# An attention and MLP chain on one core: h = x2 @ w_in by one level of Strassen's scheme

## The chip, the cores and the metric

The kernel runs on one core of one Trainium2 chip. The metric is the device time of one execution in microseconds; a time is the median over several executions. A profile is taken of one execution, which has a time of its own.

## The reference, cut to what matters

```python
# attention: 32 heads (4 batches x 8), 576 tokens, head size 64, causal, with a cumulated bias
scores = q @ k.T / 8 + minimum(bias, 0);  attn = softmax(scores);  x = attn @ v    # x: 2304 x 512
c  = (x @ w1) * (x @ w2)              # 2304 x 1024
x2 = (c @ w3) @ w_out                 # 2304 x 512, w3 1024 x 1024, w_out 1024 x 512
h  = x2 @ w_in                        # 2304 x 2048, w_in 512 x 2048
g  = h - tanh(h)
out = g @ w_out2                      # 2304 x 512, w_out2 2048 x 512
```

All inputs are float64 in memory.

## The kernel before, in words

Every engine's instruction order is written out by a planner inside the program: `pl.op` notes an operation with the engines that may run it, its reads, its writes and a priority (a lower number is taken first); `order` plays the list through with assumed costs and puts each operation on an engine; `emit` then issues all in that order. On the chip each engine runs its instructions in order and waits on semaphores. The assumed costs, the biases and the priorities are in `PARAM`. All DMAs are issued from SP's queue (L392).

**Precision.** A float32 product is made of three matmuls on "fp32r" operands: each operand is split (`split`, L404) into a rounded high part (`copy`: ScalarE L395 or VectorE L396) and a low part (`sub`: VectorE L399 or GpSimd L401), and high*high, high*low and low*high are added in a bank. So a block of 128 rows, depth 128 and n columns costs three matmuls of n columns. A float64 weight tile of 128x512 is turned into float32 by `assemble` (L490: one ScalarE or VectorE operation, L495 or L496, then L497, L498, L500 and L502 on VectorE); `convert` does that and splits, `lay_by` does that and writes the float32 tile to DRAM, `fetch` brings it back and splits.

**Stages.** (1) The heads (L621), with the products x @ w1 and x @ w2 (`products`, L791; c goes to DRAM) in between as filler: block j of 512 tokens may run when its heads are done. (2) w3 @ w_out (L865 to L875, eight rounds of 24 matmuls, `wah` and `wal` are its result), after the conversions of 8 tiles of w_out and 16 of w3. The first six rounds (`wlast=6`) have a priority ahead of the remaining products. (3) x2 = c @ (w3 w_out) (L890 to L917) in five blocks of tokens, four of 512 and one of 256: c is loaded (`cf`) and split, and each block takes 4 banks of 24 matmuls. Its result is split out of PSUM and written to DRAM as high and low parts. In the same stretch the 16 tiles of w_in are converted into `wih` and `wil`, which stay in SBUF, and those of w_out2 into `voh` and `vol`. (4) h and out (L925 to L974): five blocks of tokens as before; for each of 16 slices f of 128 columns of h there are 12 matmuls into one of 4 banks (L945), then the gate g = h - tanh(h), then for each 128 tokens of the block three matmuls of 512 columns (L966 to L968) into one of the other 4 banks, one slice or more later.

The gate of a slice: ScalarE squares h out of PSUM (L953), squares again (L954), takes tanh (L955) and a mask (L958); VectorE makes h*u out of PSUM (L956), a polynomial (L957), h - tanh out of PSUM (L959), a predicated copy (L960); then the split into `gh` (L396) and `gl` (L401, GpSimd).

Of the kernel before, what the change touches and what calls it, by code (L numbers as in the profile page):

```python
# [9 lines left out]
F32 = mybir.dt.float32  # L10
# [6 lines left out]
P = 128  # L17
# [8 lines left out]
TB = 512  # L26
# [49 lines left out]
class Plan:  # L76
# [68 lines left out]
    def order(self):  # L145
# [18 lines left out]
        def better(o, e, t):  # L164
            early = t < PARAM["early"]
            bias = {"DVE": PARAM[{"sub": "dsub", "copy": "dcopy"}.get(o.kind, "dother") + ("0" if early else "")], "ACT": PARAM["act"], "POOL": PARAM["pool"]}
# [123 lines left out]
def f_mm(n, m=P):  # L290
    return [(112.0 if m > 64 else 58.0, 227.0 if n == 512 else n * 0.447 + 4.8 if n >= 96 else 30.0)]
# [6 lines left out]
def f_pair(ns):  # L298
    f = [(112.0, 0.8333 * n + 3.5) for n in ns for _ in range(2)]
    return [(f[0][0], f[0][1] + 50.0)] + f[1:-1] + [(f[-1][0], f[-1][1] + 40.0)]  # L300
# [31 lines left out]
def tile_kernel(ctx, tc, qk, v, s, w1, w2, w3t, w_out, w_in, w_out2, out):  # L332
# [49 lines left out]
    x2_d = Buf(len(XT) * KC)  # L382
    x2_d.t = dram.tile([P, 2, KC, NT], F32, name="x2_d")

    wt_d = Buf(NF2)
# [12 lines left out]
    def sub(dst, a, b, n, r, w, prio, psum=False):  # L398
# [3 lines left out]
        pl.op(o, r=r, w=w, prio=prio, two=not psum, kind="sub")  # L402

    def split(hi, hb, lo, lb, src, n, r, prio, psum=False):  # L404
        copy(hi, src, n, r, [hb], prio, psum)
        sub(lo, src, hi, n, r + [hb], [lb], prio, psum)
# [60 lines left out]
    wip = Pool("wip", "left")  # L467
    wih = wip.buf("wih", [P, KC, DF2], F32R, n=16)
    wil = wip.buf("wil", [P, KC, DF2], F32R, n=16)
    cp = Pool("cp", "right")  # L470
    cf_r = cp.ring("cf", PARAM["ncf"], [P, 512])
    x2s_r = cp.ring("x2s", 3, [P, 2, 512], F32R, n=2)
# [4 lines left out]
    voh = [(pre if f < NPRE else p2).buf(f"voh{f}", [P, DM], F32R) for f in range(NF2)]  # L477
    vol = [(pre if f < NPRE else p2).buf(f"vol{f}", [P, DM], F32R) for f in range(NF2)]
    x2b = [q_.buf(f"x2b{i}", [P, 2, KC, BLK], F32R) for i, q_ in enumerate((pre, p2))]
    gh_r = p2.ring("gh", PARAM["ng"], [P, BLK], F32R)  # L480
    gl_r = p2.ring("gl", PARAM["ng"], [P, BLK], F32R)
    u_r = p2.ring("u", 2, [P, BLK])
    sq_r = p2.ring("sq", 2, [P, BLK])
    th_r = p2.ring("th", 2, [P, BLK])
    pg_r = p2.ring("pg", 2, [P, BLK])
    mk_r = p2.ring("mk", 1, [P, BLK])
# [3 lines left out]
    def assemble(src, prio, first=None, after=()):  # L490
        r_, t_ = raw_r.next(), t1_r.next()
# [18 lines left out]
    def lay_by(i, src, prio, after=()):  # L510
        t_ = assemble(src, prio, None, after)
        dma(lambda: wt_d.t[i], lambda: t_.t.bitcast(F32), P * 2048, [t_], [(wt_d, i)], prio)
# [7 lines left out]
    keep.open()  # L520
    w12.open()
    abp.open()
# [313 lines left out]
    products(0)  # L836
    for b in range(1, B):
# [6 lines left out]
        if b == B - 1:  # L844
# [3 lines left out]
            wtmp.open()  # L848
        for j in range(NB):
            if b * S < min((j + 1) * TB, NT) <= (b + 1) * S:  # L850
                products(j)
    abp.close()
    w12.close()
    wip.open()


# [164 lines left out]
```

## Time and profile before

| what | value |
|---|---|
| median of 3 executions | 930.7 us (930.68 to 930.79) |
| the profiled execution | 931.48 us |
| its span, first to last instruction | 929.8 us |
| TensorE busy / weight loads | 921.6 us (99%) / 765.1 us (82%) |
| VectorE, ScalarE, GpSimd busy | 700.5 us (75%), 426.6 us (46%), 377.8 us (41%) |
| data moved | 115.36 MB, 124 GB/s over the span |

Busy time of TensorE counts each matmul from its start to a modelled end, and matmuls overlap, so a busy engine may still be issuing more slowly than it could. The distance from start to start is what one costs. VectorE's instructions overlap a little as well.

### The profile page before, as it was taken

What the parts mean: (1) busy time and instruction counts of PE and PEld (TensorE: products, weight loads), DVE (VectorE), ACT (ScalarE), POOL (GpSimd) and SP (SyncE); (2) the same over time, 40 slices, a digit from 0 to 9 for tenths busy, and PEclk for the clock granted to TensorE, in tenths of its full rate; (3) what the DMA queues carried; (4) which work ended last, traced back from release to release, by engine and by line L of the source; (5) the groups of instructions that cost most, each with busy time, mean ns of one, the idle gap of its engine ahead of it and who ended that gap; (6) DMA issues with size and microseconds to landing.
All of it is one profiled execution on the core that took longest, in us unless ns stands there. A gap on an engine that the chain in (4) does not pass through costs nothing.

```text
span 929.8 us, 14217 instructions
## 1 busy us (share of the span) xinstructions
PE 921.6 (99%) x5007; PEld 765.1 (82%) x5007; DVE 700.5 (75%) x1485; ACT 426.6 (46%) x952; POOL 377.8 (41%) x309
## 2 busy tenths in 40 slices
PE   9999999999999999999999999999999999999998
PEld 7777878888887888899888988888888888888887
DVE  8999897876664299996789999997556655656665
ACT  7857565655551022211423275554444444444353
POOL 2256765545342044414978544452222222222221
PEclk9999999999999999999999999999999999999999
DMA  7666646654421144477897652221020001100010
GB/s 226 183 199 181 201 146 205 213 160 135 131 84 49 56 147 155 164 233 240 284 326 247 227 176 68 75 107 46 1 91 15 31 1 46 46 1 0 1 47 23
DMA packets 58888, 115.36 MB, mean 124 GB/s; under 512 B 5713, under 2 KB 24305, under 8 KB 58818
## 3 DMA queue, kind: packets, MB, share of 16 engines
q1 hardware_dynamic: 58818, 114.47, 38.6%
q8 instruction: 39, 0.64, 0.3%
q14 instruction: 31, 0.25, 0.1%
HBM read 85.30 MB, written 25.46 MB: 119 GB/s over the span
## 4 chain that ended last, share of the span: by engine, by line
PE 92%; DVE 4%; POOL 1%; issue 1%; ACT 1%; DMA 1%; POOLq 0%; DVEq 0%
PE bank L945 21%; PE bank L806 20%; PE bank L966 7%; PE bank L967 7%; PE bank L968 7%; PE bank L725 5%; PE bank L752 4%; PE bank L908 4%; PE bank L909 4%; PE bank L907 4%; PE bank L670 2%; PE bank L671 2%; PE bank L668 2%; PE bank L872 1%; PE bank L871 1%; PE bank L870 1%
## 5 line engine op out<-in xcount | busy, mean ns | idle before, releaser
L401 POOL TENSOR_TENSOR gl<-pg,gh 128x512 fp32r<-128x512 f32 (+1 forms) x78 | 99.2, 1272 | 260.9 <-DVE gh L396 249.0
L945 PE MATMUL bank<-x2b,wih 128*128 128x512 f32 (+1 forms) x640 | 181.3, 368 | 0.0
L945 PEld LDWEIGHTS bank<-x2b,wih 128*128 128x128 f32 x640 | 117.0, 188 | 21.2
L958 ACT ACTIVATE mk<-u,const 128x512 f32<-128x512 f32 (+1 forms) x80 | 54.5, 681 | 142.5 <-DVE pg L960 142.4
L945 PE MATMUL bank<-x2b,wil 128*128 128x512 f32 (+1 forms) x320 | 117.7, 368 | 0.0
L966 PE MATMUL bank<-voh,gh 128*128 128x512 f32 x288 | 112.2, 390 | 0.0
L967 PE MATMUL bank<-vol,gh 128*128 128x512 f32 x288 | 112.2, 390 | 0.0
L968 PE MATMUL bank<-voh,gl 128*128 128x512 f32 x288 | 112.0, 389 | 0.0
L691 ACT ACTIVATE e<-e,nmx 128x576 f32<-128x576 f32 (+4 forms) x160 | 89.2, 559 | 39.7 <-DVE nmx L685 38.8
L956 DVE TENSOR_TENSOR pg<-bank,u 128x512 f32<-128x512 f32 (+1 forms) x80 | 50.9, 636 | 42.3 <-POOL gl L401 42.3
L685 DVE CUSTOM_DVE_ANT_0 e<-bank,msk 128x288 f32<-128x288 f32 (+4 forms) x160 | 64.3, 422 | 16.5 <-PE bank L671 14.2
L725 PE MATMUL bank<-ident,e 128*128 128x128 f32 (+1 forms) x480 | 75.4, 276 | 0.6 <-ACT e L691 0.3
L396 DVE CAST gh<-pg 128x512 fp32r<-128x512 f32 (+1 forms) x77 | 30.5, 396 | 52.8 <-PE bank L967 52.6
L945 PEld LDWEIGHTS bank<-x2b,wil 128*128 128x128 f32 x320 | 60.3, 188 | 9.9
L401 POOL TENSOR_TENSOR xl<-cf,xh 128x512 fp32r<-128x512 f32 (+1 forms) x40 | 53.3, 1360 | 34.2 <-DVE xh L396 32.3
L953 ACT ACTIVATE u<-bank 128x512 f32<-128x512 f32 (+1 forms) x80 | 43.7, 546 | 50.4 <-PE bank L945 42.3
L395 ACT ACTIVATE en<-bank 128x256 f32<-128x256 f32 (+3 forms) x97 | 40.9, 427 | 52.2 <-PE bank L725 42.3
L495 ACT ACTIVATE wt<-wraw 128x512 f32<-128x512 f32 x54 | 36.4, 673 | 59.4 <-DMA wraw<-w_in 26.7
L968 PEld LDWEIGHTS bank<-voh,gl 128*128 128x128 f32 x288 | 54.1, 188 | 11.4
L966 PEld LDWEIGHTS bank<-voh,gh 128*128 128x128 f32 x288 | 54.2, 188 | 10.8
L967 PEld LDWEIGHTS bank<-vol,gh 128*128 128x128 f32 x288 | 54.1, 188 | 10.5
L806 PE MATMUL bank<-xh,w1h 128*128 128x512 f32 (+1 forms) x160 | 62.7, 392 | 0.0
(134 smaller groups left out, 2280.2 us busy)
## 6 DMA issues: line engine op xcount, KB each, us to landing
rqk<-qk SPq DMA_DIRECT2D x24, 576.0 KB
wraw<-w_out SPq DMA_DIRECT2D x24, 512.0 KB
wraw<-w SPq DMA_DIRECT2D x16, 512.0 KB
c_d<-cst SPq DMA_DIRECT2D x32, 256.0 KB
wraw<-w3t SPq DMA_DIRECT2D x16, 512.0 KB
wraw<-w_in SPq DMA_DIRECT2D x16, 512.0 KB
cf<-c_d SPq DMA_DIRECT2D x32, 256.0 KB
x_d<-x2s SPq DMA_DIRECT2D x16, 512.0 KB
```

The source lines that it names most:

```text
L401: o.append(("POOL", c_pool2(n), lambda: nc.gpsimd.tensor_tensor(dst(), a(), b().bitcast(F32), op=ALU.subtract)))
L685: nc.vector.tensor_tensor_reduce(e.t[:nq, EOFF[t] + k0:EOFF[t] + k1], bk.t[:nq, :k1 - k0], bi.t[:nq, bo + k0:bo + k1], -0.125, 3.0e38 if f ...
L691: act(lambda: nc.scalar.activation(et(), et(), AF.Exp, bias=nmx.t[:nq, i, tm:tm + 1], scale=-1.0, accum_out=ssum.t[:nq, pj, t, i:i + 1]), ...
L725: nc.tensor.transpose(bk.t[:rows, (at + m) * P:(at + m + 1) * P], e.t[:, EOFF[t] + c * P:EOFF[t] + c * P + rows], ident.t)
L806: nc.tensor.matmul(bk.t[:, :w], w_.t[:, k, f * P:(f + 1) * P], x_.t[:, k, :w], start=k == 0 and i == 0, stop=k == KC - 1 and i == 2)
L945: nc.tensor.matmul(bk.t[:, :w], w_.t[:, k, a], X2.t[:, i, k, :w], start=k == 0 and n == 0, stop=k == KC - 1 and n == 2)
L953: act(lambda u=u, hp=hp, c_=c_: nc.scalar.activation(c_(u), hp(), AF.Square), w, [bk], [u], pr, psum=True)
L956: dve(lambda u=u, pg=pg, hp=hp, c_=c_: nc.vector.tensor_tensor(c_(pg), hp(), c_(u), op=ALU.mult), w, [bk, u], [pg], pr)
L958: act(lambda u=u, mk=mk, c_=c_: nc.scalar.activation(c_(mk), c_(u), AF.Relu, bias=const.t[:, 1:2]), w, [u, const], [mk], pr, extra=93.0)
L966: nc.tensor.matmul(bank[n].t, gh.t[:, a], voh[f].t, start=f == 0, stop=False)
L967: nc.tensor.matmul(bank[n].t, gh.t[:, a], vol[f].t, start=False, stop=False)
L968: nc.tensor.matmul(bank[n].t, gl.t[:, a], voh[f].t, start=False, stop=f == NF2 - 1)
```

## The change

The products of h are taken over pairs of 384-token blocks (three pairs of 768 tokens). For such a pair, the depth 512 of x2 is cut in two, the 2048 columns of w_in in two, and the tokens in two; the eight block products become seven (Winograd's form of Strassen's scheme). The operands of a product are sums and differences of quarters. In detail:

- **w_in.** Its 16 tiles are put into float32 and laid by in DRAM (`wi_d`) with a priority behind the heads, and later read back, added and subtracted, split (56 splits of 128x256) and written to `ws_d`. That is spread over the eight rounds of w3 @ w_out (`weights(i)`). In the h stage each step loads its seven operands, 256 KB each, into a ring `ws` of 13.
- **x2.** Six blocks of 384 tokens in place of five; its result leaves PSUM as it is. The operands of the first pair are made at once (8 differences, 14 splits); x2 of the other pairs goes to DRAM (`xf_d`), is read back in the h stage (`later_x2`), combined, split and written to `x2_d`, and loaded again.
- **h and out.** A step (3 pairs x 8) makes seven products of 6 matmuls of 384 columns, issued in pairs (0 and 1, 2 and 3, 4 and 5, then 6), with the 9 out matmuls of a tile of the step before between them. Two banks hold products (three in the first step), six hold out. Sums of products are partly made in PSUM (a product is added to a bank that has been read) and partly by VectorE: five additions out of PSUM and two copies a step. The gate runs on 128x384 tiles in SBUF, four a step; h*u, h - tanh and the low part may go to VectorE or GpSimd.
- **Order.** `wlast` is 0 (all of w3 @ w_out behind the products x @ w1, x @ w2), no tile of w_out2 is laid by, 12 of its 16 tiles have buffers from before the h stage (4 so far), the rings `gh` and `gl` have 8 buffers of 384 columns (3 of 512 so far), the staging buffers of the products are used again for `cf` and for the sums, and the numbers of `PARAM` differ throughout. The planner's matmul cost is n / 2.4 + 13 ns.

```diff
-BLK = 512
-HT = [(t, min(t + BLK, NT)) for t in range(0, NT, BLK)]
-XT = [(t, min(t + 512, NT)) for t in range(0, NT, 512)]
+XB = 384
+XT = [(t, t + XB) for t in range(0, NT, XB)]
+ORDER = (0, 5, 1, 6, 4, 3, 2)
...
+    for n in range(NF2):
+        c, kg, m = n // 8, n // 4 % 2, n % 4
+        j, i = ((0, 0), (0, 1), (1, 1), (1, 0))[m]
+        k, qd = j * 2 + kg, c + 2 * i
+        lay_by(wi_d, k * 4 + qd, w_in[k * P:(k + 1) * P, qd * 512:(qd + 1) * 512], PARAM["layw"] + 10 * n)
...
+
+        def lay(i, x):
+            for m in range(2):
+                st = wst_r.next()
+                split(lambda st=st: st.t[:, :, 0], (st, 0), lambda st=st: st.t[:, :, 1], (st, 1),
+                      lambda m=m: v_(x).rearrange("p (f x) -> p f x", x=P)[:, m * 2:m * 2 + 2], 256, [x], pr, kind="late")
+                dma(lambda m=m: ws_d.t[c * 4 + m * 2:c * 4 + m * 2 + 2, :, i, kg].rearrange("f p h x -> p f h x"), lambda st=st: st.t.bitcast(F32), P * 2048,
+                    [st], [(ws_d, c * 14 + i * 2 + kg)], pr, row=1024, issue=600.0)
...
+        if part == 0:
+            a11, a21 = unit(0, 0), unit(0, 1)
+            lay(0, a11)
+            s3 = made(a11, a21)
+            lay(6, s3)
+            held_w[:] = [a11, a21, s3]
+        else:
+            a11, a21, s3 = held_w
+            a22 = unit(1, 1)
+            lay(3, a22)
+            s1 = made(a21, a22, ALU.add, a21)
+            lay(4, s1)
+            s2 = made(s1, a11, to=a11)
+            lay(5, s2)
+            a12 = unit(1, 0, s3)
+            lay(1, a12)
+            lay(2, made(a12, s2, to=a12))
...
+            x = (xd_r if p else xs_r).next()
+            held[l, d] = x
+            copy(lambda x=x, d=d: x.t, lambda d=d: bks[d].t[:, :XB], XB, [bks[d]], [x], 1.9e5, psum=True)
+            if p:
+                dma(lambda d=d: xf_d.t[p, l, d], lambda x=x: x.t, P * XB * 4, [x], [(xf_d, (p * 2 + l) * KC + d)], 2.2e5, row=1536, issue=580.0)
...
+        b11, b12, b21, b22 = b
+        lay(0, b11)
+        lay(1, b21)
+        lay(2, b22)
+        lay(4, made(b12, b11, b11))
+        lay(6, made(b22, b12, b12))
+        t2 = made(b22, b11)
+        lay(5, t2)
+        lay(3, made(b21, t2, b21))
...
+
+        def lay(i, x):
+            st = x2s_r.next()
+            split(lambda: st.t[:, 0], (st, 0), lambda: st.t[:, 1], (st, 1), lambda: x.t, XB, [x], pr, kind="xs")
+            dma(lambda: x2_d.t[p, i, :, kg], lambda: st.t.bitcast(F32), P * 2 * XB * 4, [st], [(x2_d, p * 14 + i * 2 + kg)], pr, issue=580.0)
+
+        operands(kg, b, xt_r, pr, lay)
...
+
+        def product(n, i, bk, first):
+            def mm():
+                for kg in range(2):
+                    for m, (a, z) in enumerate(((0, 0), (0, 1), (1, 0))):
+                        nc.tensor.matmul(bk.t[:, :XB], W[i].t[:, kg, a], X[i].t[:, kg, z], start=first and kg == 0 and m == 0, stop=kg == 1 and m == 2, skip_group_check=True)
...
+
+        def plus(bk, y):
+            x, v_ = tmp()
+            dve(lambda: nc.vector.tensor_tensor(v_(), bk.t[:, :XB], y[1](), op=ALU.add), XB, [bk, y[0]], [x], -1.0e6)
+            return x, v_
+
...
+            def both(o, i, a, r, w):
+                pl.op([("DVE", c_dve(XB), lambda: nc.vector.tensor_tensor(o.t, i(), a.t, op=ALU.mult if o is pg else ALU.subtract)),
+                       ("POOL", c_pool2(XB), lambda: nc.gpsimd.tensor_tensor(o.t, i(), a.t, op=ALU.mult if o is pg else ALU.subtract))], r=r, w=w, prio=pr, two=True, kind="gate")
+            act(lambda: nc.scalar.activation(u.t, h(), AF.Square), XB, [hb], [u], pr)
+            act(lambda: nc.scalar.activation(sq.t, u.t, AF.Square, bias=const.t[:, 0:1], scale=SQ_A), XB, [u, const], [sq], pr, extra=93.0)
+            act(lambda: nc.scalar.activation(th.t, h(), AF.Tanh), XB, [hb], [th], pr)
+            both(pg, h, u, [hb, u], [pg])
+            dve(lambda: nc.vector.scalar_tensor_tensor(pg.t, sq.t, SQ_K, pg.t, op0=ALU.add, op1=ALU.mult), XB, [sq, pg], [pg], pr, two=True)
+            act(lambda: nc.scalar.activation(mk.t, u.t, AF.Relu, bias=const.t[:, 1:2]), XB, [u, const], [mk], pr, extra=93.0)
+            both(th, h, th, [hb, th], [th])
+            dve(lambda: nc.vector.copy_predicated(pg.t, mk.t.bitcast(U32), th.t), XB, [mk, th], [pg], pr, two=True)
+            copy(lambda: gh.t, lambda: pg.t, XB, [pg], [gh], pr)
+            sub(lambda: gl.t, lambda: pg.t, lambda: gh.t, XB, [pg, gh], [gl], pr, psum=last, kind="gate")
+            for n in range(3):
+                o = bank[l * 3 + n]
+
+                def om(n=n, o=o):
                     a = slice(n * P, (n + 1) * P)
+                    nc.tensor.matmul(o.t, gh.t[:, a], voh[f].t, start=fp == 0 and f == fp + l * NFP, stop=False)
+                    nc.tensor.matmul(o.t, gh.t[:, a], vol[f].t, start=False, stop=False)
+                    nc.tensor.matmul(o.t, gl.t[:, a], voh[f].t, start=False, stop=fp == NFP - 1 and f == fp + (1 - l) * NFP)
+                pe(f_op(3 * f_mm(512)), om, [gh, gl, voh[f], vol[f]], [o], 2.0e6 + pos + PARAM["outlag"] + n_tile[0] % 4 * 40 + n * 12)
+            n_tile[0] += 1
...
+        product(0, 0, a, True)
+        m1 = taken(a)
+        product(1, 5, b, True)
+        u2 = plus(b, m1)
+        product(2, 1, a, False)
+        h11 = taken(a)
+        gated(h11, fp, 0)
+        product(3, 6, b, False)
+        u3 = plus(b, m1)
+        c = h_r[0].next()
+        product(4, 4, c, True)
+        h22 = plus(c, u3)
+        gated(h22, fp + NFP, 1)
+        product(5, 3, b, False)
+        h21 = plus(b, m1)
+        gated(h21, fp + NFP, 0)
+        product(6, 2, c, False)
+        h12 = plus(c, u2)
+        gated(h12, fp, 1)
```

## Rows read from the trace of the kernel before

**Rows 1.** The page: its head and the busy time of the engines.

```profile
span 929.8 us, 14217 instructions
PE 921.6 (99%) x5007; PEld 765.1 (82%) x5007; DVE 700.5 (75%) x1485; ACT 426.6 (46%) x952; POOL 377.8 (41%) x309
```

**Rows 2.** The page: the chain that ended last, shares of the span by engine.

```profile
PE 92%; DVE 4%; POOL 1%; issue 1%; ACT 1%; DMA 1%; POOLq 0%; DVEq 0%
```

**Rows 3.** The chain in order of time, h and out: start, length, what (us).

```profile
691.60 2.72 PE bank L945 x12
697.04 2.72 PE bank L945 x12
...
893.58 1.43 PE bank L945 x12
896.40 1.43 PE bank L945 x12
```

**Rows 4.** Groups by shape, TensorE: count | busy, mean | idle before.

```profile
L945 PE MATMUL bank<-x2b,wih 128*128 128x512 f32 x512 | 157.7, 389 | 0.0
...
L966 PE MATMUL bank<-voh,gh 128*128 128x512 f32 x288 | 112.2, 390 | 0.0
...
L909 PE MATMUL bank<-xh,wal 128*128 128x512 f32 x128 | 49.8, 389 | 0.0
...
L945 PE MATMUL bank<-x2b,wih 128*128 128x256 f32 x128 | 23.6, 282 | 0.0
...
L909 PE MATMUL bank<-xh,wal 128*128 128x256 f32 x32 | 9.1, 283 | 0.0
```

**Rows 5.** Busy time by stretch: columns as its head line names them, GB/s last.

```profile
150.00:292.00 142.00, 142.00 (x954) 117.03 (x953) 96.73 (x314) 75.83 (x223) 62.91 (x60) 1.00 0.48 146
292.00:323.00 31.00, 31.00 (x138) 25.65 (x137) 8.03 (x13) 0.47 (x1) 2.90 (x3) 1.00 0.16 60
323.00:433.00 110.00, 109.90 (x570) 94.30 (x569) 100.23 (x176) 24.79 (x40) 40.27 (x28) 1.00 0.59 190
433.00:532.00 99.00, 99.00 (x488) 84.14 (x487) 81.40 (x108) 31.55 (x53) 75.90 (x56) 1.00 0.78 257
549.00:866.00 317.00, 317.00 (x1403) 262.55 (x1402) 221.25 (x344) 151.17 (x259) 95.91 (x69) 1.00 0.12 40
```

**Rows 6.** Timeline of VectorE in the h stage: start, length (us), instruction.

```profile
565.91 1.51 DVE L497 TENSOR_SCALAR wt<-wt 128x512 f32<-128x512 f32 x1
567.35 0.68 DVE L956 TENSOR_TENSOR pg<-bank,u 128x512 f32<-128x512 f32 x1
567.95 0.68 DVE L959 TENSOR_TENSOR th<-bank,th 128x512 f32<-128x512 f32 x1
...
569.14 0.42 DVE L498 TENSOR_SCALAR wt<-wt 128x512 uint32<-128x512 uint32 x1
569.48 0.76 DVE L960 COPY_PREDICATED pg<-mk,th 128x512 f32<-128x512 uint32 x1
570.12 0.69 DVE L500 SCALAR_TENSOR_TENSOR wt<-wraw,wt 128x512 uint32<-128x512 uint32 x1
```

**Rows 7.** Timeline of GpSimd in the same stretch.

```profile
565.52 1.62 POOL L401 TENSOR_TENSOR gl<-pg,gh 128x512 fp32r<-128x512 f32 x1 [1.42 <-DVE gh L396]
```

**Rows 8.** Groups by shape, operations of the gate: mean ns of one.

```profile
L401 POOL TENSOR_TENSOR gl<-pg,gh 128x512 fp32r<-128x512 f32 x64 | 88.8, 1388 | 228.6 <-DVE gh L396 219.0 <-ACT gh L395 9.6
...
L954 ACT ACTIVATE sq<-u,const 128x512 f32<-128x512 f32 x64 | 46.3, 723 | 2.7 <-DVE pg L957 2.3
L959 DVE TENSOR_TENSOR th<-bank,th 128x512 f32<-128x512 f32 x64 | 44.2, 690 | 6.5 <-ACT th L955 5.0
...
L401 POOL TENSOR_TENSOR gl<-pg,gh 128x256 fp32r<-128x256 f32 x14 | 10.4, 740 | 32.3 <-DVE gh L396 30.1 <-PE bank L945 2.2
...
L954 ACT ACTIVATE sq<-u,const 128x256 f32<-128x256 f32 x16 | 8.2, 512 | 0.1
...
L959 DVE TENSOR_TENSOR th<-bank,th 128x256 f32<-128x256 f32 x16 | 6.7, 420 | 5.4 <-ACT th L955 5.4
```

More of the change, by code (lines that the diff above doesn't have):

```diff
@@ L520, in tile_kernel @@
     keep.open()
+    abp.open()
     w12.open()
-    abp.open()
     xp.open()
@@ L918, in tile_kernel @@
+    x_r = Ring(x2b)
+    X0 = {i: x_r.next() for i in ORDER}
+    for j in range(len(XT)):
+        x2_block(j)
+    for i in range(NPRE):
+        out_weights(i)
     cp.close()
@@ new lines, in tile_kernel, with later_x2 @@
+    for i in range(NPRE, NF2):
+        out_weights(i)
+    w_r, h_r, n_tile = Ring(ws), [Ring(bank[5:8])], [0]
+    def later_x2(p, kg, pr):
+        b = []
+        for z, y in ((0, 0), (0, 1), (1, 0), (1, 1)):
+            x = xt_r.next()
+            b.append(x)
+            dma(lambda x=x: x.t, lambda z=z, y=y: xf_d.t[p, y, z * 2 + kg], P * XB * 4, [(xf_d, (p * 2 + y) * KC + z * 2 + kg)], [x], pr, row=1536)
+        def lay(i, x):
[3 more added lines that the diff above has]
+        operands(kg, b, xt_r, pr, lay)
@@ new lines, in step, with tmp, taken, gated @@
+    def step(p, fp, pos, X, W):
+        pr, last = 3.0e5 + pos, p == NPAIR - 1 and fp == NFP - 1
+        def product(n, i, bk, first):
+            def mm():
+                for kg in range(2):
+                    for m, (a, z) in enumerate(((0, 0), (0, 1), (1, 0))):
+                        nc.tensor.matmul(bk.t[:, :XB], W[i].t[:, kg, a], X[i].t[:, kg, z], start=first and kg == 0 and m == 0, stop=kg == 1 and m == 2, skip_group_check=True)
+            pe(f_op(6 * f_mm(XB)), mm, [W[i], X[i]], [bk], 2.0e6 + pos + n // 2 * 45 + n % 2)
+        def tmp():
+            x = tmp_r.next()
+            return x, lambda: x.t[:, :XB]
+        def plus(bk, y):
+            x, v_ = tmp()
+            dve(lambda: nc.vector.tensor_tensor(v_(), bk.t[:, :XB], y[1](), op=ALU.add), XB, [bk, y[0]], [x], -1.0e6)
+            return x, v_
+        def taken(bk):
+            x, v_ = tmp()
+            copy(v_, lambda: bk.t[:, :XB], XB, [bk], [x], -1.0e6, psum=True)
+            return x, v_
+        def gated(src, f, l):
+            hb, h = src
@@ new lines, in step @@
+        gated(h21, fp + NFP, 0)
+        product(6, 2, c, False)
+        h12 = plus(c, u2)
+        gated(h12, fp, 1)
+        if fp == NFP - 1:
+            for l in range(2):
+                for n in range(3):
+                    ob, t0, bk = osb_r.next(), p * 2 * XB + l * XB + n * P, bank[l * 3 + n]
+                    for a, z in ((0, 256), (256, 512)) if last else ((0, 512),):
+                        copy(lambda ob=ob, bk=bk, a=a, z=z: ob.t[:, a:z], lambda bk=bk, a=a, z=z: bk.t[:, a:z], z - a, [bk], [(ob, int(a > 0))] if last else [ob], pr, psum=True)
+                    dma(lambda t0=t0: out[t0:t0 + P, :], lambda ob=ob: ob.t, P * DM * 4, [ob], [], 0)
@@ new lines, in tile_kernel @@
+    for p in range(NPAIR):
+        if p < NPAIR - 1:
+            for kg in range(2):
+                later_x2(p + 1, kg, 3.0e5 + p * NFP * 160 + PARAM["x2p"])
+        X = X0 if p == 0 else {}
+        for i in ORDER if p else ():
+            X[i] = x_r.next()
+            dma(lambda x=X[i]: x.t.bitcast(F32), lambda i=i, p=p: x2_d.t[p, i], P * 4 * XB * 4, [(x2_d, [p * 14 + i * 2, p * 14 + i * 2 + 1])], [X[i]], 3.0e5 + p * NFP * 160, issue=600.0)
+        for fp in range(NFP):
+            pos = (p * NFP + fp) * 160.0
+            if p == 0 and fp == 1:
+                h_r[0] = Ring(bank[6:8])
+            W = {}
+            for n, i in enumerate(ORDER):
+                W[i] = w_r.next()
+                dma(lambda x=W[i]: x.t.bitcast(F32), lambda i=i, fp=fp: ws_d.t[fp, :, i], P * 2048, [(ws_d, [fp // 4 * 14 + i * 2, fp // 4 * 14 + i * 2 + 1])], [W[i]], 3.0e5 + pos + n * 20, row=2048)
+            step(p, fp, pos, X, W)
```

220 lines of the change are left out of this document (109 added, 111 removed).

## The prediction

> **What bounds the kernel now.** I read the page first: TensorE is busy for 921.6 of 929.8 us [rows 1], and the chain that ended last is TensorE for 92% of its length [rows 2]. So I ask of every edit what it does to TensorE's issue, and of all other engines only whether they come late. Busy time does not say what a matmul costs, since lengths overlap (mean 389 ns at 512 columns [rows 4]). The chain in order of time does: in h and out twelve matmuls of 512 columns take 2.72 us, the next twelve of that line start 5.44 us after the first (12 of h, 12 of out), so one costs 226.7 ns; twelve of 256 columns take 1.43 us, 119.2 ns each [rows 3]. Third, the stretches: TensorE has hardly a gap after 150 us, at a granted clock of 1.00 throughout. VectorE is busy 97 of 142 us, then 8 of 31, 100 of 110, 81 of 99, and in the h stage 221 of 317 us. ScalarE has room everywhere, the DMA share is 0.78 at most and 0.12 in the h stage [rows 5].
>
> **The change: h on TensorE.** Before, h is 64 groups of twelve at 2.72 us and 16 at 1.43 us [rows 3] (the two thirds of them that read `wih` count 512 and 128 [rows 4]): 174.1 + 22.9 = 197.0 us. After, it is 3 pairs x 8 steps x 7 products x 6 = 1008 matmuls of 384 columns. That shape is not in the trace. A line through the two that are (0.42 ns a column and 11.7 ns each) gives 172.9 ns, in all 174.3 us: **22.7 us less**. The bounds are 384 columns at the 512 rate (170.0 ns: 171.4 us, 25.6 less) and at the 256 rate (178.8 ns: 180.2 us, 16.8 less). I take the line, since a fixed part per matmul explains both shapes. An eighth of the products would be 24.6 us; the shorter matmul gives 1.9 back.
>
> x2 goes from 384 matmuls of 512 columns and 96 of 256 (three lines of 128 and 32 each, as on the one shown [rows 4]) to 576 of 384: 98.5 to 99.6 us, **1.1 more** (0.6 less to 4.5 more by the same bounds). Out has the same 864 matmuls.
>
> **VectorE in the h stage.** Costs first. Back to back, two operations of 512 columns start 0.60 us apart, though each is 0.68 long; a fast one takes 0.34 to the next, a predicated copy 0.64 [rows 6]. So an operation holds VectorE for 0.09 less than its length. At 384 columns I take the mean of the lengths at 512 and 256 (0.690, 0.420 [rows 8]), 0.555, less 0.09: 0.47 us; a fast copy 0.27, a predicated copy 0.50. GpSimd's subtraction is 740 ns at 256 and 1388 at 512, waits included: about 1.0. ScalarE's square goes from 723 and 512 to 0.62 [rows 8]; its operations out of PSUM I put at 0.48, a little shorter, as an estimate from that.
>
> A step is 42 matmuls of h and 36 of out: 7.26 + 8.16 = 15.4 us of TensorE. All on VectorE, its four gates cost 4 x (3 x 0.47 + 0.50 + 0.47 for the low part + 0.27) = 10.6 us, the five additions 2.35, together 12.9. Work for the next pair (8 differences and 14 splits in 8 steps) adds 8 x 0.47 + 14 x 0.74 = 14.1 us, 1.8 a step; in the first pair the last four tiles of w_out2 (4 x 2.8 us) add 1.4. That is 16.1 us of 15.4 in the first pair, 14.7 in the second, 12.9 in the third. ScalarE can take the copies (1.1 + 0.5 of it): four gates there cost 4 x (2 x 0.62 + 2 x 0.48) = 8.8 us, the two bank copies 1.0, those copies about 3: 12.8 of 15.4. And GpSimd can work while VectorE reads PSUM, 2.35 us a step. So it fits, at 14.5 of 15.4 in the first pair before GpSimd helps: covered, but by little where before 30% was free. I charge **2 us** for the first pair.
>
> Here stands what is held against GpSimd's help. A fast operation that is 0.42 long alone is 1.51 when it meets a GpSimd subtraction, and ends 0.3 us behind it [rows 6, 7]: they exclude each other. The Trainium skill's page "SBUF — State Buffer" ("SBUF: two separate sides") says so as a rule: VectorE operations with two SBUF inputs and GpSimd's take turns on one port pair, the loser blocks fully. The gate of before reads h from PSUM in two of its operations; now h lies in SBUF and these join the excluded ones. What that can come to is the first rival.
>
> **Banks.** Two banks hold products, four so far. Products go in pairs with nine out matmuls (2.04 us) between: a bank that is finished is written again 2.04 + 1.04 = 3.1 us later. In that time one reader of 0.48 to 0.56 us has to start and end. With some 0.2 us to pass a finish on in each direction, 1 us; 2 us are left for a queue in front of it. I charge nothing and put the failure among the rivals. The out banks of a pair are written anew only a step after their last matmul, so their six copies are covered.
>
> **Start and end.** In the first step there are no out matmuls: seven products and two of the next step, 9.3 us, have to cover the first gate, which starts at 3.1 us and is some nine dependent operations of about 0.5 us: 5 us and what it waits behind other gates. I charge **1.5 us** (0 to 4). At the end, after the last product, there are still four groups of nine, 8.2 us, for a gate of 6 us: covered; after the last matmul the copies and the DMA are as before.
>
> **w3 @ w_out.** With `wlast` 0 its eight rounds (24 matmuls, 5.44 us) come behind all products, no longer mixed with them. Each needs two conversions, of which two buffers hold only two rounds' worth. On VectorE: 2 x (2 x 0.34 + 2 x 0.60 + 0.60) + 0.60 = 5.6 us a round, six rounds: 1 us late; if GpSimd takes the low parts at 1.39 and shuts VectorE out, 7.1, 10 us late. I charge **2 us** (0 to 10). The sums of w_in cost VectorE at most 56 x 0.33 + 16 x 0.60 = 28 us, w_out2's eight more conversions 20, x2's first pair 14: 62 us. What leaves this stretch is 16 conversions of w_in (30 us without the splits) and 20 low parts and some high parts out of PSUM (about 15): 17 more, and 27 us are free from 323 to 532 us [rows 5]. Its DMA: by the sizes of the tiles 8.4 MB of w_in and 9.4 of x2 go, 14.7 and 4.2 for w_in's sums and 3.1 for x2 come: 4 MB more. At 257 GB/s for a share of 0.78, 330 at full, that is 13 us on the 142 that 0.59 of 110 and 0.78 of 99 us are, of 209.
>
> **Moved into the heads:** 16 tiles laid by, 16 x 1.88 = 30 us of VectorE and 32 DMAs on SP behind those of the heads by priority. From 150 to 323 us VectorE has 68 us free [rows 5], and TensorE has the products to run: nothing, and if the heads come late, up to 2.
>
> **The loads of the h stage:** seven tiles of 256 KB a step are 1.8 MB in 15.4 us, 119 GB/s, where 257 GB/s ran at a share of 0.78 [rows 5]; the ring holds six tiles ahead, some 13 us. At a pair's change 5.5 MB of x2 come as well: with the weights 7.3 MB, 22 us at 330 GB/s, behind buffers that come free one by one; the first is loaded ahead and the last is wanted 27 us on. Nothing.
>
> **Sum:** 931.5 - 22.7 + 1.1 + 2 + 1.5 + 2 = 915.4 us for a profiled execution; the median of the runs lies 0.8 below that of the profiled one (930.7 to 931.5), so **914.6 us**.
>
> **Rivals.** (a) VectorE and GpSimd become the bound of the h stage, and it ends slower. It decides where a step reaches 16.2 us: 24 x 0.75 is the gain of 18 that the other terms leave. If GpSimd takes the 12 movable operations of a step at 1.0 and each shuts VectorE out for 0.9, the excluded work is 10.8 + 4 x (0.47 + 0.50 + 0.27) + 1.8 = 17.6 us, in the third pair 15.8: 16 x 2.2 + 8 x 0.4 = 38 us, **950 us**. For it: no free room in the first pair; against it: ScalarE and VectorE alone come to less than 15.4 in two pairs of three. 0.10. (b) The readers of the two banks come late by more than the 2 us that are left, now and then: 0.1 us on each of four handovers in 24 steps is 10 us, **924 us**. For it: in-order queues with operations of 1 us in front. 0.14. (c) The conversions hold up w3 @ w_out and so x2 (10 instead of 2) and the first step (4 instead of 1.5): **925 us**. 0.12. (d) The gain is eaten up and the time is the same: 0.04. (e) My case, 906 to 920: 0.60.
>
> **Numbers.** About 0.2% (1.9 us) is what a measurement of this kernel can tell from no change. Faster: (e), (b), (c) less a little, 0.85; same 0.04; slower 0.11. The range goes from all terms at their good ends (384 columns at the 512 rate and no stall, 905) to (b) or (c) with a little of the other, 930.
>
> **What would show it.** Right: in the h stage six matmuls of a product in 1.04 us, a step in 15.4 to 15.7 us, x2 as long as before, h and out together some 374 us for 393. Wrong: TensorE waiting for VectorE's sums or for `gh` and `gl` in every step (a, b), VectorE above 95% there; TensorE waiting for `w3h` around 390 to 430 us (c); gaps before 150 us, if the laid-by tiles hurt the heads; a matmul of 384 columns dearer than 173 ns.

## The result

The changed kernel takes 921.5 us (median of 4 runs, 920.9 to 921.9) where the kernel before takes 930.7 in the same comparison: a ratio of 0.990, 95% interval 0.988 to 0.992. It is faster, inside the range, and 6.9 us above the predicted 914.6. The profiled execution took 921.88 us with a span of 920.2.

The page of the changed kernel, its head, its busy times and the chain by engine (for [rows 1] and [rows 2]):

```profile
span 920.2 us, 15850 instructions
PE 906.6 (99%) x5174; PEld 790.6 (86%) x5174; DVE 790.7 (86%) x1884; ACT 549.0 (60%) x1292; POOL 112.1 (12%) x106
...
PE 89%; DVE 5%; DMA 3%; ACT 1%; issue 1%; SPq 0%; ACTq 0%; DVEq 0%
```

TensorE is still the bound. VectorE went from 75 to 86%, ScalarE from 46 to 60%, GpSimd from 41 to 12%. The stretches (for [rows 5]: time busy of PE, PEld, DVE, ACT, POOL, then clock, DMA share, GB/s) show where:

```profile
150.00:292.00 142.00, 142.00 (x939) 115.95 (x937) 132.71 (x403) 54.74 (x167) 66.25 (x58) 1.00 0.60 185
...
547.00:866.00 319.00, 319.00 (x1589) 287.12 (x1588) 280.62 (x579) 235.99 (x499) 0.00 (x0) 1.00 0.66 214
```

The laid-by tiles of w_in fill VectorE in the heads (133 of 142 us, 97 before) without a gap on TensorE. In the h stage VectorE is busy 281 of 319 us and GpSimd never. All that TensorE's list of waits names after 300 us is this (us in total, times, longest):

```profile
PE bank L1055 <- DMA ws<-ws_d: 1.3, 1, 1.3
PE bank L1055 <- DVE asb L1064: 1.1, 1, 1.1
PE bank L1055 <- ACT xd L410: 0.4, 1, 0.4
```

Three waits, all between the first product of h and the first matmul of out. The chain in order of time shows one later step, products in runs of 12, 12, 12 and 6 matmuls of 384 columns (for [rows 3]):

```profile
762.87 2.08 PE bank L1055 x12
...
767.04 2.10 PE bank L1055 x12
...
771.23 2.10 PE bank L1055 x12
...
776.09 1.06 PE bank L1055 x6
...
778.55 2.08 PE bank L1055 x12
```

A step is 15.68 us (762.87 to 778.55). Between the runs stand nine matmuls of out: 764.95 to 767.04 is 2.09 us for them. Uniform stretches of the same trace give 173.3 ns for 384 columns and 226.7 for 512, so 12 should take 2.08, nine 2.04, six 1.04, and the step 42 x 173.3 + 36 x 226.7 = 15.44. The matmuls that follow a change of width take longer, though nothing is waited for. By these rows (each run to the start of the next) the 36 matmuls of out take 8.34 us for 8.16 and the 42 of h 7.34 for 7.28: most of the excess lies on out.

From the starts of TensorE's stages in the two traces:

| stretch | before | after | difference | predicted |
|---|---|---|---|---|
| start to first matmul of h | 532.29 | 532.83 | +0.5 | +1.1 (x2), +2 (w3 @ w_out) |
| first of h to last matmul of out | 393.08 | 379.57 | -13.5 | -22.7, +1.5 (first step), +2 (first pair) |
| last matmul to end of span | 4.47 | 7.77 | +3.3 | 0 |
| sum | 929.84 | 920.17 | -9.7 | -16.1 |

Sixty matmuls of h stand before the first of out, which comes 14.21 us after the first of h: 10.4 us of work and 3.8 lost. Before there were 72 at 226.7 ns in 16.35 us, nothing lost.

The chain through the first step and the timeline of ScalarE at the end:

```profile
537.70 0.61 DVE wt L522
...
538.33 0.33 SPq L407
...
538.72 4.99 DMA ws<-ws_d
...
543.84 3.36 PE bank L1055 x18
```

```profile
909.42 1.34 ACT L410 ACTIVATE osb<-bank 128x256 f32<-128x256 f32 x4 [2.37 <-PE bank L1097]
912.24 1.35 ACT L410 ACTIVATE osb<-bank 128x256 f32<-128x256 f32 x4 [1.48 <-DMA out<-osb]
915.06 1.40 ACT L410 ACTIVATE osb<-bank 128x256 f32<-128x256 f32 x4 [1.46 <-DMA out<-osb]
```

At the start, SP issues a load of w_out2 (538.33) once VectorE has freed its buffer (L522, 537.70), and only behind it the operands of the next products (`ws`); the first of them lands at 543.7, and TensorE, which has issued seven products by then, waits for it. (The seven operands of the first step were issued by 500.4.) At the end two output tiles are copied out, then the copies wait 1.5 us until a tile's DMA has landed, twice.

### The profile page after: what moved, and what is told of

The parts are those of the page before. It is cut to its first block, busy times and chain, and to the rows that moved or that the text cites. A ratio compares the mean times of both kernels' runs of the same rounds, so it can differ in the third digit from the quotient of the medians.

```text
span 920.2 us, 15850 instructions
## 1 busy us (share of the span) xinstructions
PE 906.6 (99%) x5174; PEld 790.6 (86%) x5174; DVE 790.7 (86%) x1884; ACT 549.0 (60%) x1292; POOL 112.1 (12%) x106
## 4 chain that ended last, share of the span: by engine, by line
PE 89%; DVE 5%; DMA 3%; ACT 1%; issue 1%; SPq 0%; ACTq 0%; DVEq 0%
PE bank L826 21%; PE bank L1055 18%; PE bank L1096 7%; PE bank L1097 7%; PE bank L1095 7%; PE bank L745 5%; PE bank L772 5%; PE bank L979 2%; PE bank L978 2%; PE bank L980 2%; PE bank L690 2%; PE bank L688 2%; PE bank L691 2%; PE bank L941 2%; PE bank L942 2%; PE bank L943 2%
## 5 line engine op out<-in xcount | busy, mean ns | idle before, releaser
L1055 PE MATMUL bank<-x2b,ws 128*128 128x384 f32 x1008 | 192.9, 337 | 2.8 <-DMA ws<-ws_d 1.3
L1055 PEld LDWEIGHTS bank<-x2b,ws 128*128 128x128 f32 x1008 | 178.8, 188 | 12.1 <-DVE asb L1064 3.0
L711 ACT ACTIVATE e<-e,nmx 64x64 f32<-64x64 f32 (+4 forms) x160 | 89.1, 558 | 95.6 <-DVE nmx L705 95.0
L705 DVE CUSTOM_DVE_ANT_0 e<-bank,msk 64x64 f32<-64x64 f32 (+4 forms) x160 | 64.7, 420 | 4.5 <-PE bank L691 3.9
L980 PE MATMUL bank<-xh,wal 128*128 128x384 f32 x192 | 64.1, 334 | 0.0
L978 PE MATMUL bank<-xh,wah 128*128 128x384 f32 x192 | 64.1, 334 | 0.0
L979 PE MATMUL bank<-xl,wah 128*128 128x384 f32 x192 | 64.1, 334 | 0.0
L826 PE MATMUL bank<-xh,w2h 128*128 128x512 f32 (+1 forms) x160 | 63.3, 396 | 0.0
L826 PE MATMUL bank<-xh,w1l 128*128 128x512 f32 (+1 forms) x160 | 59.4, 371 | 0.0
L1087 DVE COPY_PREDICATED pg<-mk,th 128x384 f32<-128x384 uint32 x96 | 57.8, 602 | 1.9
```

The costliest lines, as they stand in the source:

```text
L705: nc.vector.tensor_tensor_reduce(e.t[:nq, EOFF[t] + k0:EOFF[t] + k1], bk.t[:nq, :k1 - k0], bi.t[:nq, bo + k0:bo + k1], -0.125, 3.0e38 if f ...
L711: act(lambda: nc.scalar.activation(et(), et(), AF.Exp, bias=nmx.t[:nq, i, tm:tm + 1], scale=-1.0, accum_out=ssum.t[:nq, pj, t, i:i + 1]), ...
L826: nc.tensor.matmul(bk.t[:, :w], w_.t[:, k, f * P:(f + 1) * P], x_.t[:, k, :w], start=k == 0 and i == 0, stop=k == KC - 1 and i == 2)
L978: nc.tensor.matmul(bk.t[:, :XB], wah.t[:, f, a], ch, start=f == 0, stop=False)
L979: nc.tensor.matmul(bk.t[:, :XB], wah.t[:, f, a], cl, start=False, stop=False)
L980: nc.tensor.matmul(bk.t[:, :XB], wal.t[:, f, a], ch, start=False, stop=f == NF - 1)
```

## The experiments

Twelve kernels were run, in four groups, each with the kernel before beside it, which lay at 930.5 to 931.1. Where no interval is given, the time is of one execution.

**The end's buffers.**

```diff
-    cst_r = abp.ring("cst", 3, [P, TB])
-    asb_r = abp.ring("asb", 4, [P, TB])
+    cst_r = abp.ring("cst", 3, [P, TB], n=2)
+    asb_r = abp.ring("asb", 4, [P, TB], n=2)
...
-                    ob, t0, bk = osb_r.next(), ...
+                    ob, t0, bk = (tmp_r if last else osb_r).next(), ...
```

> The last step's six out tiles are staged in six of the seven buffers that held the sums of the products, in place of the ring of two. Theory (the end of the changed kernel, 7.8 us from the start of the last matmul to the end of the span where it was 4.5 before, waits for the DMA of an earlier out tile to land before a staging buffer is free): the end falls to 4.5 to 5.0 us, the time to 918.2 to 918.8 us. Rival (the end is long because ScalarE makes all twelve half copies of the last block alone, 0.34 us each): nothing is gained by buffers, 7.5 us and more, 921.2 to 921.8.

919.15 us (918.7 to 919.3), ratio 0.988 (0.986 to 0.989): the end falls as the theory said, and the time lies 0.4 us above its range. ScalarE's timeline at the end:

```profile
909.75 2.02 ACT L410 ACTIVATE cst<-bank 128x256 f32<-128x256 f32 x6 [2.38 <-PE bank L1097]
911.79 2.02 ACT L410 ACTIVATE asb<-bank 128x256 f32<-128x256 f32 x6
```

The twelve copies run without a wait, and the span ends 4.83 us after the last matmul and not 7.77, as before the change (4.47). The ring of two tiles cost 2.9 of the 3.3 us.

**The order of the loads at the start.** Three of the last four conversions of w_out2 are created after the weight loads of the second step and wait for them.

```diff
-    for i in range(NPRE, NF2):
-        out_weights(i)
+    out_weights(NPRE)
...
+            if p == 0 and fp == 1:
+                for i in range(NPRE + 1, NF2):
+                    out_weights(i, [W[n] for n in ORDER])
```

> The last three conversions of w_out2 are put behind the weight loads of the second step on SP's queue. Theory (the first out matmul comes 14.2 us after the first product of h, where ten products make 10.4 us; 1.4 of the 3.8 us are a wait for a weight tile whose load stands behind a load of w_out2 that waits for VectorE to free its buffer): 12.2 to 13.0 us to the first out matmul and 920.0 to 920.6 us. Rival 1 (the copies and sums of the first step come late because VectorE and ScalarE are full, whatever SP's queue does): 13.8 to 14.2 us, 921.3 to 921.8. Rival 2 (both): 10.4 to 11.5 us and 918.5.

933.5 us (932.8 to 935.8), ratio 1.004 (1.002 to 1.005): slower than before. At the start almost nothing changed (3.6 us lost for 3.8), and the edit did not clear SP's queue there: the conversion that was not moved has its load in the same place, with ten loads of `ws` behind it.

```profile
537.66 0.33 SPq L407 DMA_DIRECT2D wraw<-w_out  x1
538.04 5.85 SPq L407 DMA_DIRECT2D ws<-ws_d  x10
```

The third wait of the start is now for a sum of VectorE (1.1 us). In the changed kernel VectorE's last sum before that matmul ends at 543.4, 0.3 us before the load lands, so that the load alone would be worth little if this is the sum awaited.

A new wait of 10.5 us for `ws` came at 579.5. The chain there, and what SP waits for from 570 to 592 us:

```profile
575.96 0.61 DVE wt L522
576.59 4.56 DMA wraw<-w_out
...
584.88 5.14 DMA ws<-ws_d
590.07 1.97 PE bank L1054 x5
```

```profile
SPq L407 <- DVE x2s L414: 4.9, 4, 2.9
SPq L407 <- DVE xt L879: 4.1, 1, 4.1
SPq L407 <- DVE wt L522: 2.3, 3, 1.8
```

Two of the moved loads stand on SP among the loads and writes of the next pair's x2 (`xt`, `x2s`). Both kinds wait for VectorE, which is full there (26.0 of 26.0 us from 550 to 576) and now has the moved conversions in its order as well: 9.0 us of SP's waits are for its work on x2, 2.3 for buffers of w_out2. The operands `ws` behind them are issued only from 584.9. Whether the order of the loads made the slow start, this run does not decide. It shows that an issue that waits for VectorE holds up all that stands behind it on SP.

**Without the late conversions.**

```diff
-    for i in range(NPRE):
+    for i in range(8):
         out_weights(i)
+    for i in range(8, NF2):
+        voh[FO[i]], vol[FO[i]] = voh[FO[i - 8]], vol[FO[i - 8]]
...
-    for i in range(NPRE, NF2):
-        out_weights(i)
```

> Leaves out the conversion of 8 of the 16 tiles of w_out2; out uses the other 8 twice. Theory (the conversions, on SP's queue, ScalarE and VectorE, cost the first step its 3.8 us): the first out matmul comes 10.4 to 11.2 us after the first product of h and the time is 918.0 to 918.8 us. Rival (the loads of the second step's weights, which start only when x2's buffers are free, and the length of the first gate): 13 to 14.2 us, 920.5 to 921.8. A rival of the prediction (VectorE is the bound of the first pair, whose steps should then get shorter without the conversions): steps of the first pair below 15.6 us; the theory says 15.67 as they are.

918.2 us. Out begins 12.61 us after h, between the theory and the rival, with 66 matmuls ahead of it (11.4 us): 1.2 lost and not 3.8. One wait is left, and VectorE stays nearly full in the first pair:

```profile
PE bank L1055 <- DVE asb L1064: 0.7, 1, 0.7
```

```profile
550.00:600.00 50.00, 50.00 (x250) 44.85 (x249) 49.14 (x105) 38.53 (x84) 0.00 (x0) 1.00 0.70 219
```

So 2.6 of the 3.8 us come from the eight conversions left out. The steps of the first pair are 15.67 us with and without them, as are those of the third pair, where VectorE has less to do: that it is 49.9 of 50 us busy in the first pair of the changed kernel costs nothing.

**One width.**

```diff
-                    nc.tensor.matmul(o.t, gh.t[:, a], voh[f].t, ...)
-                    nc.tensor.matmul(o.t, gh.t[:, a], vol[f].t, ...)
-                    nc.tensor.matmul(o.t, gl.t[:, a], voh[f].t, ...)
+                    o_ = o.t[:, :XB]
+                    nc.tensor.matmul(o_, gh.t[:, a], voh[f].t[:, :XB], ...)
+                    nc.tensor.matmul(o_, gh.t[:, a], vol[f].t[:, :XB], ...)
+                    nc.tensor.matmul(o_, gl.t[:, a], vol[f].t[:, :XB], ...)
+                    nc.tensor.matmul(o_, gl.t[:, a], voh[f].t[:, :XB], ...)
```

> The matmuls of out take 384 columns, as those of h do, and four in place of three make a group (the low part of g times the low part of w_out2 is added); the last 128 columns of out are left out. A step is then 42 + 48 = 90 matmuls of 384 columns. Theory (the 0.25 us by which a step of 15.67 us is over 42 x 173.3 + 36 x 226.7 ns come from the changes between 384 and 512 columns, eight in a step): no excess, 15.60 us a step, every matmul 173 to 174 ns, the time 919.5 to 920.0 us. Rival (they come from the change of operands, banks or waits between h and out): the excess stays, 15.80 to 15.90 us a step, 925 to 927 us.

919.1 us. The chain in order of time:

```profile
777.05 2.08 PE bank L1055 x12
...
781.21 2.08 PE bank L1055 x12
...
790.23 1.04 PE bank L1055 x6
...
792.65 2.08 PE bank L1055 x12
```

Twelve products' matmuls take 2.08, six 1.04, twelve of out 2.08, the step 15.60: all 90 at 173.3 ns. With the same gates, sums and loads around them, the excess is gone when the widths are equal; and where all had 512 columns, before the change, twelve of h and twelve of out took 5.44 us, 24 x 226.7 ns [rows 3]. It belongs to the change of width.

**One product more.**

```diff
         product(6, 2, c, False)
+        product(6, 2, c, False)
```

> One product of every step (the one of w part 2) is issued twice into its bank, so the second half of the output is wrong there; six matmuls of 384 columns more in each of 24 steps. Theory (a product is paid in full on TensorE, nothing else sets the h stage's pace): six matmuls at 173.3 ns = 1.04 us a step, so the step goes from 15.67 to 16.71 us and the time from 921.5 to 946.5 us (24 x 1.04 = 25.0). Rival (part of a step is slack behind VectorE or ScalarE, so that a product left out by the scheme is worth less than its matmuls): a step grows by less than 0.9 us, and the time is below 943.

945.45 us, 23.9 more than the changed kernel. The chain (runs of 12 now four times a step):

```profile
777.12 2.08 PE bank L1055 x12
...
790.34 2.10 PE bank L1055 x12
...
793.84 2.08 PE bank L1055 x12
```

The step is 16.72 (777.12 to 793.84), 1.04 more. Every product is paid in full; 24 x 1.04 = 25.0, of which the first step gives 1.3 back, since the added product fills part of its waits (2.5 lost and not 3.8).

**GpSimd in the gates.**

```diff
-                pl.op([("DVE", c_dve(XB), lambda: ...),
-                       ("POOL", c_pool2(XB), lambda: ...)], ...)
+                pl.op([("POOL", c_pool2(XB), lambda: ...)], ...)
```

> The two subtractions or products of each gate that could go to either engine are put on GpSimd (8 of a step, 192 in all); nothing is left out. Rival (a) of the prediction, tried on purpose: if VectorE and GpSimd exclude each other here, 8 operations of about 1 us shut VectorE out for some 7 to 8 us a step while it loses 8 x 0.47 = 3.8 us of its own work: VectorE, at 25 of 25 us in the first pair and 20 of 25 in the third, would need about 19 us a step in the first pair and 16 in the third, TensorE would wait in each step, and the time would be 930 to 1000 us. If they do not exclude each other, VectorE's busy time in the h stage falls by a quarter, steps stay at 15.67 us, and the time is 919 to 923.

947.45 us, 25.9 above the changed kernel. Groups by shape on VectorE from 550 to 650 us (count | busy, mean ns), first with the gates on GpSimd, then the changed kernel:

```profile
L1086 DVE COPY_PREDICATED pg<-mk,th 128x384 f32<-128x384 uint32 x25 | 22.7, 909 | 0.6
L1083 DVE SCALAR_TENSOR_TENSOR pg<-sq,pg 128x384 f32<-128x384 f32 x25 | 20.5, 822 | 0.0
...
L414 DVE TENSOR_TENSOR gl<-pg,gh 128x384 fp32r<-128x384 f32 x25 | 14.9, 597 | 0.1
L414 DVE TENSOR_TENSOR x2s<-xt,x2s 128x384 fp32r<-128x384 f32 x16 | 12.4, 778 | 0.0
L1064 DVE TENSOR_TENSOR asb<-bank,cst 128x384 f32<-128x384 f32 x21 | 11.6, 553 | 3.3 <-PE bank L1055 3.1
```

```profile
L1087 DVE COPY_PREDICATED pg<-mk,th 128x384 f32<-128x384 uint32 x27 | 16.3, 605 | 0.0
L1084 DVE SCALAR_TENSOR_TENSOR pg<-sq,pg 128x384 f32<-128x384 f32 x27 | 15.0, 557 | 0.0
...
L1064 DVE TENSOR_TENSOR asb<-bank,cst 128x384 f32<-128x384 f32 x20 | 11.2, 558 | 0.0
L414 DVE TENSOR_TENSOR x2s<-xt,x2s 128x384 fp32r<-128x384 f32 x17 | 9.4, 554 | 0.0
```

Three of VectorE's operations on SBUF operands grow from 605 to 909, 557 to 822 and 554 to 778 ns, while the additions that read PSUM stay at 553 to 558. (The low part `gl` grows from 557 only to 597.) This is what the Trainium skill's page "SBUF — State Buffer" ("SBUF: two separate sides") says: VectorE operations with two SBUF inputs and GpSimd's hold one port pair in turn. The trace agrees for the first three; what spares `gl`, no run here shows. A later window of this run (TensorE's busy time first, the clock third from the end):

```profile
650.00:700.00 50.00, 35.44 (x148) 30.80 (x147) 42.96 (x68) 32.86 (x70) 26.77 (x22) 0.78 0.75 260
```

The price fell in one stretch and not in every step: from 640 to 705 us, around the change to the next pair, TensorE waited 15.7 us (8.0 of it for VectorE's sums, 5.4 for a late tile of w_out2), and after the waits its clock was at the lower level of 1.2 GHz for some of the time (0.78 in the mean). From 705 us on the steps are 15.67 again. So rival (a) is a real mechanism, but that 947 lies near its 950 is chance: it was priced for twelve operations and a loss in every step. The changed kernel does not meet it, because its list puts none of the gates' work on GpSimd.

**Two attempts at earlier conversions**, both with the end's buffers.

```diff
-            convert(..., 3.5e5 + 10 * i)
+            convert(..., 2.5e5 + (1.5 + 0.35 * i if i < NPRE else 1.0e5 + 10 * i))   # first
+            convert(..., (2.4e5 if i < NPRE else 3.5e5) + 10 * i)                    # second
```

> The version that the runs so far point to: the output tiles of the last step go to the idle buffers (2.4 us less, as in the run with the tail's buffers), and the first twelve conversions of w_out2 get a priority among those of x2's operands, so that they are issued between 436 and 515 us, where VectorE is idle half the time, and not between 515 and 546. Nothing is left out. Theory (the conversions of that time delay the start of h by the 2.6 us that leaving out eight of them brought): the time falls to 916 to 917.5, out begins about 12.6 us after h with ten or eleven products in front. Rival (another order moves a wait elsewhere: x2 waits for its operands, or SP's queue holds a load back): the start gains 2 us and x2 or a step of the first pair loses as much, 918 to 922.

> As the run beside it, but the twelve conversions come ahead of all of x2's operands in priority and not among them. Theory: 916 to 917.5 as well, if x2's operands, which then stand behind the conversions, still come in time. Rival: x2 (432.9 to 532.8) begins or runs later by what the conversions take from VectorE, up to 5 us, and the time is 919 to 922.

927.1 us (926.4 to 927.3), ratio 0.996 (0.994 to 0.997), and 928.5 us (927.7 to 929.7), ratio 0.997 (0.996 to 0.998). h starts at 543.0 and 543.6 and not at 533. TensorE's waits from 440 to 560 us and the busiest window of the first of the two:

```profile
PE bank L979 <- DVE xl L414: 6.4, 3, 4.0
```

```profile
510.00:530.00 20.00, 14.94 (x69) 13.80 (x70) 19.90 (x42) 11.10 (x22) 0.00 (x0) 0.83 0.71 231
```

VectorE splits x2's last operands behind the conversions, x2 waits 6.4 us, and TensorE's granted clock is 0.83 in the mean of that window. The rival held in kind, but h starts 10 us late where 2 to 5 were named, and both times lie above its range. That VectorE is half idle from 450 to 500 us (24 of 50 us busy) did not help.

**Eight or four tiles laid by in the heads**, with the end's buffers.

```diff
+    lay = FO[8:]          # FO[12:] in the third
+    for n, f in enumerate(lay):
+        lay_by(wt_d, f, w_out2[f * P:(f + 1) * P, :], PARAM["layw"] + 160 + 10 * n)   # 2.05e5 in the second
     for b in range(1, B):
```

> A version again, nothing left out: the last step's output tiles go to the idle buffers (2.4 us, measured), and eight tiles of w_out2 are assembled and written out during the heads, behind the sixteen of w_in, and only loaded, copied and subtracted at the start of the h stage: 256 KB and two operations there for 512 KB and six. That takes 8 x 2.1 us of VectorE out of the crowded 500 to 565 us without an operation more in front of x2's operands. Theory: out begins some 12.6 us after h, as with eight conversions left out, and the time is 916 to 917.5. Rival (VectorE, at 47 of 50 us from 150 to 300 us, has no room for 8 x 1.9 us more during the heads): w3 @ w_out begins or x2's first matmul (433.0 us) comes up to 5 us later, and the time is 918 to 922.

> The same, with the eight tiles laid by at a lower priority, just behind the conversions of w_out and before those of w3. Theory: they then take room from 300 to 350 us, where VectorE has 13 of 50 us free, and the heads stay as they are: 916 to 917.5. Rival: w3's conversions come later by them and TensorE waits before 433 us: 919 to 922.

> The same as the first of the three, with four tiles and not eight. Theory: half of the gain at the start, 917 to 918.5; rival (the heads have no room): half of its loss, 918 to 920.

919.2 us (918.8 to 920.2), 922.8 (921.7 to 923.9) and 921.9 (921.7 to 922.2): the first in its rival's range, the others above both of theirs. In the first, 2.5 us are lost in the first step for 3.8, but h starts 2.3 us later than with the end's buffers alone (535.34 for 533.05). What the start gains is lost before, though not as the rival had it: x2's first matmul is on time (432.5), but TensorE waits 1.3 us for copies between the products, and twelve matmuls of w3 @ w_out (2.8 us) are left for behind x2's first twelve. In the other two TensorE's list names no wait from 300 to 433 us; it waits for x2's splits (2.0 and 1.5 us) and for the copies of x2's last banks (3.0 and 0.8). No version beat the end's buffers alone.

**The rounds of w3 @ w_out as before.**

```diff
-             wap=1402502, ...
-             wlast=0, ...
+             wap=721486, ...
+             wlast=6, ...
```

> One part of the change undone: the first six rounds of w3 @ w_out go ahead of the remaining products again, with the priority that they had before (wlast 6, wap 721486); nothing is left out. Theory (in the changed kernel TensorE has no wait between 300 and 533 us, so the order of the rounds and the products is worth nothing): x2's first matmul starts within 1 us of 433.0 and the time is 920.5 to 923. Rival (the late rounds are what keeps the stretch free of waits, as the charge of 2 us for them supposed a stall in the other direction): TensorE waits for w3's conversions, x2 starts 2 to 6 us later, 924 to 928; if the late rounds themselves cost the 0.7 us by which x2 now starts later, the time falls by that, to 920.8.

936.4 us (935.5 to 938.2), ratio 1.006 (1.004 to 1.007): 14.9 us above the changed kernel, slower than before. Theory and size both fell. TensorE's waits from 432 to 460 us:

```profile
PE bank L978 <- ACT xh L410: 13.0, 1, 13.0
```

and ScalarE's splits of x2's first operands on the timeline, first this kernel, then the changed one:

```profile
431.76 0.52 ACT L410 ACTIVATE xh<-asb 128x384 fp32r<-128x384 f32 x1 [1.36 <-PE bank L826]
...
448.02 0.52 ACT L410 ACTIVATE xh<-cst 128x384 fp32r<-128x384 f32 x1
```

```profile
400.48 0.51 ACT L410 ACTIVATE xh<-asb 128x384 fp32r<-128x384 f32 x1
...
428.22 0.52 ACT L410 ACTIVATE xh<-cst 128x384 fp32r<-128x384 f32 x1
```

x2's operands go into `xb`, which the products x @ w1 and x @ w2 read to their end, and c passes through buffers that the products use too, so that most of these splits come behind the products. In the changed kernel the products end at 400.3, and 32 us of w3 @ w_out cover the splits. With six rounds moved forward TensorE has 2.7 us of them left behind the last product (432.6 us) and then stands still from 435.5 to 448.6, where x2 starts; in the changed kernel it starts at 433.0. What stretches the splits over 16 us (431.8 to 448.0) is not c's way alone. The chain through this wait runs over the sums of w_in, which belong to the same rounds:

```profile
433.94 4.14 DMA ws_d<-wst
...
439.43 3.53 DMA ws_d<-wst
...
443.89 3.65 DMA ws_d<-wst
```

Three writes of split sums to DRAM, one behind the other, make 11.3 us of it. ScalarE and VectorE have the splits of w_in's sums and those of c in one order, and SP the transfers of both. No run takes the two apart.

## Why the prediction was right in direction and 7 us off

- **h on TensorE, 22.7 us less.** Right in mechanism: every product is paid in full (the added one). The terms that were mis-sized are the price of a matmul of 384 columns ("172.9 ns, in all 174.3 us") and "Out has the same 864 matmuls", which was charged nothing: both prices hold where all matmuls have one width (173.3 and 226.7 ns), not where runs of the two widths alternate. The step is 15.67 for 15.42 us: 24 x 0.25 = **6.0 us more**, of which 5.6 are the change of width and 0.4 the 173.3. Most of the 5.6 lies on out and not on h, so the bound of 178.8 ns for 384 columns (5.9 us) covered the sum by luck. The one-width run shows the cause.
- **The end: "after the last matmul the copies and the DMA are as before".** Wrong, **3.3 us more**: six tiles are now finished within the last 3.5 us and have two output buffers. The buffers alone bring back 2.9.
- **First step, 1.5 us.** Measured 3.8, **2.3 more**, inside its range of 0 to 4. 2.6 of the 3.8 are conversions of w_out2; whether they act through VectorE or through SP's order, no run tells apart. With them gone, 1.2 are lost, near the 1.5 charged.
- **First pair, 2 us for VectorE.** Measured nothing, **2 less**. VectorE was even fuller than estimated (49.9 of 50 us for 14.5 of 15.4), and TensorE did not wait for it once after the first step. Being full was not yet being late.
- **Before h, 3.1 us.** Measured 0.5, **2.6 less**. x2's own matmuls cost 1.2 more, as forecast (99.7 us for 98.5; before, 1.4 us of a product stand among them). The stall charged with 2 for the rounds of w3 behind the products did not come: TensorE has no wait from 300 to 533 us, and with the rounds mixed again, in this kernel, the time is 15 us longer. In the kernel before, mixed rounds cost no such wait (x2 starts at 432.3).
- Together 6.0 + 3.3 + 2.3 - 2 - 2.6 = 7.0 of the 6.9. The terms of h and out come to -22.7 + 6.0 + 3.8 = -12.9 for -13.5 measured; 0.6 us stay unassigned. That the total is off by 7 and not by 11.6 is luck: two terms were too high by 4.6.
- **Charged nothing, rightly:** the two product banks (no wait on a sum after the first step, so rival (b) did not happen), the laid-by tiles in the heads, and the loads (share 0.66 for 0.12 in the h stage, one wait of 1.3 us, counted with the first step).
- **Rivals.** (a) did not come, since GpSimd does nothing in this h stage; when made to, 947. (c) gave the first step's part alone. The measured 921.5 lies inside the range but 1.5 us above the band of "my case, 906 to 920".
- **Signs.** The step came in its band (15.4 to 15.7), with six matmuls at 1.04 to 1.06 us; h and out together took 379.6 us and not 374. VectorE above 95% was named as a sign of being wrong and came true in the first pair without a wait: the sign was badly chosen.

What is not settled: why a load of w_out2 could not be brought forward into the idle VectorE time between 450 and 500 us. Both attempts by priority and all three by laying by moved other operations with it, since the whole order is planned anew; an order that changes only these conversions was not tried. Nor is it settled whether the load in front of `ws` on SP at 538 us costs the first step anything, and how much of the 15 us with mixed rounds is c's way into x2 and how much w_in's sums.

## What to carry to other kernels

When matmuls are made fewer, price them in the mix in which they will run: runs of different widths in turn cost more than the sum of uniform runs. Look at the last tiles as at a stage of its own: work that used to end one tile after another may now end all at once, with too few buffers to leave. And before a filler is moved, ask what else passes under it: here six rounds of weights, put behind the products, covered c's way through DRAM and the sums of w_in, and moving them forward cost 15 us.

## What the runs showed of the hardware that had not been expected

After a run of 384-column matmuls, the first nine of 512 columns take about 2.08 us in all and not 2.04, and the first six of 384 after nine or twelve of 512 take 1.06 us and not 1.04; the tenth to twelfth of a run of 512 are at 226.7 again. After only six of 512 the run of 384 has its uniform price (2.08 for twelve, at 762.87 and 778.55). It is the same in every step of the second and third pairs and is gone when all matmuls have one width. What in TensorE causes it, no run here shows.
